# Stores on the ACT queue, group 3 ahead of group 2, and a reordered opening in a chunked-attention and squared-ReLU kernel

## The chip, the cores and the metric

The kernel runs on one core of one Trainium2 chip. The metric is device time in microseconds (us) of one launch, the median of several. A core has five engines that run beside each other, each through its own instructions in order: TensorE (PE, matmul and transpose into PSUM; PEld is its weight load), VectorE (DVE), ScalarE (ACT), GpSimd (POOL) and SyncE (SP). A DMA is issued from an engine's instruction stream (here SP or ACT) and then moved by 16 DMA engines. An instruction that waits for a semaphore holds up everything behind it on its engine.

## The reference

```python
B, H, S, D = 8, 8, 576, 64                      # q, k, v: fp32
q_c, k_c, v_c = (a.reshape(B, H, 9, 64, D) for a in (q, k, v))
scores = D ** -0.5 * q_c @ k_c.swapaxes(-1, -2)  # 64 x 64 per chunk
attn = softmax(scores)
x = (attn @ v_c).reshape(B, H, S, D).transpose(0, 2, 1, 3).reshape(4608, 512)
h = maximum(x @ w_in, 0)                         # w_in 512 x 2048
out = (h * h) @ w_out                            # w_out 2048 x 512, out fp32 4608 x 512
```

Attention stays inside chunks of 64 tokens; a feed-forward network (FFN) with a squared ReLU follows.

## The kernel before

The 4608 tokens are 18 groups of 256, and two groups make a block of 512 (`blocks`, L40): nine blocks, 0 to 8. The order of everything is written out by hand: the program is built in the order in which the Python code calls things, and each engine runs its share of that order.

**Attention of one group** is a chain of steps with short names (L297). For groups 0 to 3, PE transposes q and k (T, `transpose_qk`, or `transpose_qk_early` at the opening), and DVE and then ACT copy the result into `qkT`. From group 4 on POOL casts q and k to bf16 (C, `cast_qk`), and a DMA transpose on SP fills `qkT` (TD, `transpose_qk_dma`, L221). Then come the scores and the exponential on ACT (SC, `scores`), the products with v and the division on DVE (AV, `values`), and the transpose of the result x into `xT` (XT, `transpose_x`; XE and `transpose_x_early` in the opening; from group 6 on it is a DMA transpose on SP, L279).

**FFN of block j** is `ffn_in(j, c, n)`: 16 tiles of columns, called ft here, of four matmuls each (L316), each followed by a ReLU on ACT (`rl`, L322) and a square on DVE (`gT`, L323). Then comes `ffn_out(j)`: four tiles of 128 tokens with 16 matmuls each (L332), and for each a copy `o_sb` on ACT (L339) and a store (L341). Block 0 uses `ffn_out_by_ft` (L352), which can start before all of w_out is there; block 1 does `ffn_in` in two halves of 256 tokens. The matmuls of the FFN write the four PSUM buffers `ps_ffn` in turn, so ft n+4 needs the buffer that the ReLU of ft n has read.

**Interleaving.** Each `yield` of these loops is a slot, counted from 0 in each block: slots 0 to 15 follow the ft of `ffn_in`, then 16 follow `ffn_out` (block 1 has 48 in all). `at(slot, f, g)` puts a step of a later group behind that slot, and one load of q, k or v is issued in each slot in `go_slots` (`loads`). So the scores of groups 2j+2 and 2j+3 stand inside block j, and their loads one or two blocks earlier.

**Queues.** SP issues every load, every DMA transpose and every store, in the order of the program. DMAs take eight completion semaphores, DMAHW0 to DMAHW7, in turn; a DMA is issued only when the DMA that had its semaphore before has landed. That wait stands on the issuing engine.

**Opening.** SP loads q, k and v of groups 0 and 1, then eight slices of w_in and eight of w_out through five staging buffers `w_st`, with a cast on POOL for each (the first slice of w_in as two halves), then groups 2 and 3. `keep_busy(n)` puts n small matmuls without use on PE. PE does T, SC, AV and XE of groups 0 and 1 before block 0.

## Time and profile before

| | us |
|---|---|
| median of 3 runs | 311.0 (310.59 to 311.77) |
| the profiled execution's own time | 308.89 |
| its span, first to last instruction | 307.1 |
| PE busy in the span | 282.2 (92%) |
| ACT busy | 131.1 (43%) |
| DVE busy | 116.0 (38%) |
| POOL busy | 49.9 (16%) |
| mean granted TensorE clock | 0.993 |

All times below are of this one execution, in us from its first instruction; 308.89 - 307.1 = 1.8 us lie outside the span. The blocks begin at 20.95 (block 0), 55.64, 94.31, 127.11, 156.49, 186.41, 216.41, 246.41 and 275.78 (block 8). A row of the timeline gives the start, the time until the last of its instructions ended, engine, line, operation, output<-input, the count and, in brackets, how long the engine sat idle before it and what ended that. "SPq" rows are SP issuing DMAs: their time is that of the issue, not of the transfer. In the rows by windows, "DMA share" is the busy time of 16 DMA engines over the window; it can pass 1.

### The profile page before, as it was taken

The page shows a single profiled execution, that of the slowest core. Times are in us where ns is not written, and L with a number is a line of the kernel's source. Part 1 is how long each engine was busy: PE and PEld are TensorE (multiplying, and loading weights), DVE is VectorE, ACT ScalarE, POOL GpSimd, SP SyncE. Part 2 cuts the span into 40 slices and gives each one's busy share as a digit, 9 for nine tenths or more (in the row PEclk, how much of TensorE's full clock was granted, in tenths as well). Part 3 has the DMA queues.
Part 4 walks back from the last instruction along what each step waited for, and adds up shares of the span by engine and source line. Part 5 has one row for each costly group of instructions (what it writes and reads, how often), then busy time and mean ns, then how long its engine had stood idle before and what let it go on. Part 6 is the DMA issues. An engine that isn't in the chain of part 4 may idle for free.

```text
span 307.1 us, 6400 instructions
## 1 busy us (share of the span) xinstructions
PE 282.2 (92%) x2576; PEld 142.1 (46%) x2610; DVE 116.0 (38%) x246; ACT 131.1 (43%) x225; POOL 49.9 (16%) x68
## 2 busy tenths in 40 slices
PE   2979969899599699999999999999999999999995
PEld 2754434677254244444444444444444444444442
DVE  1348603586053290158026602740284028104400
ACT  1346403666315641374247315631663176226511
POOL 1037830031032050014002200320041000000000
PEclk9999997999999999999999999999999999999999
DMA  7999999897989997997699979999799903210011
GB/s 208 221 308 361 370 236 226 237 202 179 236 189 232 211 216 178 248 198 157 168 244 228 162 172 278 199 142 236 190 216 149 247 36 35 70 68 36 0 68 68
DMA packets 159149, 57.04 MB, mean 186 GB/s; under 512 B 139664, under 2 KB 152464, under 8 KB 159120
## 3 DMA queue, kind: packets, MB, share of 16 engines
q1 hardware_dynamic: 159120, 56.64, 82.1%
q8 instruction: 20, 0.33, 0.5%
q14 instruction: 9, 0.07, 0.1%
HBM read 36.70 MB, written 9.44 MB: 150 GB/s over the span
## 4 chain that ended last, share of the span: by engine, by line
PE 67%; DMA 11%; SPq 7%; DVE 5%; issue 4%; ACT 3%; POOL 1%; ACTq 0%
PE ps_ffn L332 34%; PE ps_ffn L316 27%; DMA w_st<-in_moe_w_in_dram 4%; DMA k_sb<-in_k_dram 3%; DVE gT L323 3%; DMA qkT<-qkb 3%; PE ps_ffn L352 2%; ACT rl L322 2%; DMA w_st<-in_moe_w_out_dram 2%; SPq L101 2%; DVE x L266 2%; SPq L221 1%; PE ps_att L256 1%; SPq L116 1%; SPq L109 1%
## 5 line engine op out<-in xcount | busy, mean ns | idle before, releaser
L316 PE MATMUL ps_ffn<-xT,w_in_bf 128*128 128x512 bf16 (+1 forms) x619 | 128.8, 357 | 1.7 <-ACT xT L201 0.5
L323 DVE TENSOR_TENSOR gT<-rl 128x512 bf16<-128x512 bf16 (+1 forms) x160 | 78.7, 510 | 133.5 <-ACT rl L322 130.9
L332 PE MATMUL ps_ffn<-w_out_bf,gT 128*128 128x512 bf16 x501 | 111.7, 379 | 0.8 <-issue 0.3
L322 ACT ACTIVATE rl<-ps_ffn 128x512 bf16<-128x512 f32 (+1 forms) x160 | 86.9, 558 | 42.8 <-PE ps_ffn L316 33.8
L316 PEld LDWEIGHTS <-w_in_bf 128*128 128x128 bf16 x640 | 60.7, 98 | 59.7 <-DVE xT L293 0.9
L332 PEld LDWEIGHTS <-gT 128*128 128x128 bf16 x512 | 49.8, 98 | 59.1
L339 ACT COPY o_sb<-ps_ffn 128x512 f32<-128x512 f32 x32 | 18.8, 587 | 92.5 <-PE ps_ffn L332 86.8
L214 POOL CAST qkb<-q_sb 128x1024 bf16<-128x1024 f32 x14 | 15.5, 1109 | 156.0 <-DMA q_sb<-in_q_dram 96.8
L266 DVE TENSOR_TENSOR x<-ps_att,rec 128x512 bf16<-128x512 f32 x36 | 24.9, 691 | 1.2
L242 ACT ACTIVATE e<-ps_att 128x1024 bf16<-128x1024 f32 x18 | 17.9, 1026 | 11.0 <-PE ps_att L235 11.0
L214 POOL CAST qkb<-k_sb 128x1024 bf16<-128x1024 f32 x14 | 15.9, 1138 | 1.5 <-DMA k_sb<-in_k_dram 1.2
L352 PE MATMUL ps_ffn<-w_out_bf,gT 128*128 128x512 bf16 x62 | 15.7, 405 | 0.4 <-issue 0.3
L235 PE MATMUL ps_att<-qkT 64*64 64x64 bf16 x576 | 8.1, 200 | 7.2 <-DMA qkT<-qkb 5.7
L263 DVE RECIPROCAL rec<-ps_att 128x8 f32<-128x8 f32 x36 | 7.1, 198 | 16.9 <-PE ps_att L256 16.9
L138 POOL CAST w_in_bf<-w_st 128x1024 bf16<-128x1024 f32 (+1 forms) x9 | 8.7, 966 | 20.3 <-DMA w_st<-in_moe_w_in_dram 20.1
L235 PEld LDWEIGHTS <-qkT 64*64 64x64 bf16 x576 | 6.3, 112 | 12.3 <-DMA qkT<-qkb 6.9
L256 PEld LDWEIGHTS <-e 64*64 64x64 bf16 x576 | 6.6, 107 | 9.1 <-DVE x L266 3.3
L256 PE MATMUL ps_att<-ve_sb,e 64*64 64x65 bf16 x288 | 9.1, 196 | 1.7 <-DVE x L266 1.5
L352 PEld LDWEIGHTS <-gT 128*128 128x128 bf16 x64 | 6.2, 102 | 7.7 <-issue 1.0
L145 POOL CAST w_out_bf<-w_st 128x1024 bf16<-128x1024 f32 x8 | 8.7, 1087 | 3.0 <-DMA w_st<-in_moe_w_out_dram 2.7
L256 PE MATMUL ps_att<-vo_sb,e 64*64 64x65 bf16 x288 | 9.1, 196 | 0.0
L171 ACT COPY qkT<-ps_att 128x512 bf16<-128x512 bf16 x4 | 2.1, 588 | 14.4 <-DVE qkT L171 12.5
(28 smaller groups left out, 47.8 us busy)
## 6 DMA issues: line engine op xcount, KB each, us to landing
out_dram<-o_sb SPq DMA_DIRECT2D x36, 256.0 KB, 2.4
q_sb<-in_q_dram SPq DMA_DIRECT2D x25, 256.0 KB, 4.8
k_sb<-in_k_dram SPq DMA_DIRECT2D x25, 256.0 KB, 5.1
ve_sb<-in_v_dram SPq DMA_DIRECT2D x32, 128.0 KB, 3.9
vo_sb<-in_v_dram SPq DMA_DIRECT2D x32, 128.0 KB, 3.0
w_st<-in_moe_w_out_dram SPq DMA_DIRECT2D x8, 512.0 KB, 5.8
w_st<-in_moe_w_in_dram SPq DMA_DIRECT2D x7, 512.0 KB, 7.3
q_sb<-in_q_dram SPq DMA_DIRECT2D x3, 512.0 KB, 5.4
```

Of the source, the lines that this page charges most:

```text
L138: nc.gpsimd.tensor_copy(out=w_in_bf[:, :, cols], in_=st)
L214: nc.gpsimd.tensor_copy(out=qkb[:, which], in_=qk[g][which].rearrange("p t h d -> p (t h d)"))
L235: nc.tensor.matmul(out=ps[64 * c:64 * c + 64, o0:o0 + 64], lhsT=qkT[64 * a:64 * a + 64, 1, t, hp, cols], rhs=qkT[64 * a:64 * a + 64, 0, t, ...
L242: nc.scalar.activation(out=e.rearrange("p a h t q -> p (a h t q)"), in_=ps, func=AF.Exp, scale=scale)
L256: nc.tensor.matmul(out=ps[64 * p:64 * p + 64, a, hp * (D + 1):(hp + 1) * (D + 1)], lhsT=e[64 * c:64 * c + 64, a, hp, t, :], rhs=vb[64 * c: ...
L266: nc.vector.tensor_tensor(out=x.rearrange("p h a d -> p a h d"), in0=o[:, :, :, 0:D], in1=rec.to_broadcast([128, 2, n_hp, D]), op=ALU.mult)
L316: nc.tensor.matmul(out=h[:, 0:n], lhsT=w_in_bf[:, dt, ft * 128:(ft + 1) * 128], rhs=xT[:, dt, c:c + n], start=(dt == 0), stop=(dt == n_dt ...
L322: nc.scalar.activation(out=rl[:, 0:n], in_=h[:, 0:n], func=AF.Relu)
L323: nc.vector.tensor_tensor(out=gT[:, ft, c:c + n], in0=rl[:, 0:n], in1=rl[:, 0:n], op=ALU.mult)
L332: nc.tensor.matmul(out=o_ps, lhsT=gT[:, ft, tt * 128:(tt + 1) * 128], rhs=w_out_bf[:, ft, :], start=(ft == 0), stop=(ft == n_ft - 1))
L339: nc.scalar.copy(out=o_sb, in_=o_ps)
L352: nc.tensor.matmul(out=o_ps[tt], lhsT=gT[:, ft, tt * 128:(tt + 1) * 128], rhs=w_out_bf[:, ft, :], start=(ft == 0), stop=(ft == n_ft - 1))
```

## The change

Stores are issued from ACT (`nc.scalar.dma_start`) instead of SP. Block 1 is [3, 2] instead of [2, 3], so group 3 is loaded and handled first; the rows of the stores and the pieces of odd v follow. The first two slices of w_in are loaded from the ACT queue, as whole slices, between the transposes of group 1 and AV of group 0; the cast of slice 0 is still in two halves. AV of group 0 stands before SC of group 1, there are 42 instead of 66 idle matmuls, the k half of group 1 is copied on ACT instead of DVE, and `transpose_x_early` copies its second half on DVE. In block 1, 17 instead of 20 loads stand before the DMA transposes of groups 4 and 5. In block 2, SC, AV and XT of groups 6 and 7 stand two slots later (`d` from 2 to 4).

```diff
--- before.py
+++ after.py
@@ -37,7 +37,8 @@
     n_ft = d_ff // 128
     GT = 256
     n_grp = n_tokens // GT
-    blocks = [[g, g + 1] for g in range(0, n_grp, 2)]
+
+    blocks = [[0, 1], [3, 2]] + [[g, g + 1] for g in range(4, n_grp, 2)]
     FIRST_DMA_T = 4
     FIRST_DMA_X = 6
     BT = GT * max(len(b) for b in blocks)
@@ -116,7 +117,7 @@
             yield lambda t=t, p=p, m=m, b=b, s=s: nc.sync.dma_start(
                 out=v_even[g % NV][p:p + m, t, :, 0:D],
                 in_=v[b, 0::2, s:s + m, :].rearrange("h s d -> s h d"))
-        for n in ([0] if g == 0 else []) + [2 * g + 1, 2 * g + 2]:
+        for n in {0: [0, 1, 2], 2: [5], 3: [6, 7, 8]}.get(g, [2 * g + 1, 2 * g + 2]):
             lo, hi = max(0, 128 * n - 64), min(n_tokens, 128 * n + 64)
             p = lo - (128 * n - 64)
             for b, s, m in segments(lo, hi - lo):
@@ -129,13 +130,14 @@
         for f in pieces:
             f()
 
-    def load_w_in(c0, n=256):
-        cols = slice(c0, c0 + n)
-        st = wst_pool.tile([128, 1024], FP32, name="w_st")
-        st = st[:, 0:n_dt * n].rearrange("p (a f) -> p a f", a=n_dt)
-        nc.sync.dma_start(
-            out=st, in_=moe_w_in[:, cols].rearrange("(a p) f -> p a f", p=128))
-        nc.gpsimd.tensor_copy(out=w_in_bf[:, :, cols], in_=st)
+    def load_w_in(i, eng=nc.sync, n_cast=1):
+        cols = slice(i * 256, (i + 1) * 256)
+        st = wst_pool.tile([128, 1024], FP32, name="w_st").rearrange("p (a f) -> p a f", a=n_dt)
+        eng.dma_start(out=st, in_=moe_w_in[:, cols].rearrange("(a p) f -> p a f", p=128))
+        n = 256 // n_cast
+        for c in range(0, 256, n):
+            nc.gpsimd.tensor_copy(
+                out=w_in_bf[:, :, i * 256 + c:i * 256 + c + n], in_=st[:, :, c:c + n])
 
     def load_w_out(i):
         st = wst_pool.tile([128, 1024], FP32, name="w_st").rearrange("p (a f) -> p a f", a=2)
@@ -198,7 +200,8 @@
                 out=psb[:, hp * 128:(hp + 1) * 128],
                 in_=x[:, hp].rearrange("p a d -> p (a d)"),
                 identity=ident)
-        nc.scalar.copy(
+        copy = nc.vector.tensor_copy if t else nc.scalar.copy
+        copy(
             out=xTs[j][:, :, c + t * 128:c + (t + 1) * 128],
             in_=psb[:, 0:512].rearrange("p (h t) -> p h t", h=n_hp))
 
@@ -337,8 +340,8 @@
                 if ft == n_ft - 1:
                     o_sb = ffn_pool.tile([128, d_model], FP32, name="o_sb", bufs=4)
                     nc.scalar.copy(out=o_sb, in_=o_ps)
-                    t0 = blocks[j][0] * GT + tt * 128
-                    nc.sync.dma_start(out=out[t0:t0 + 128, :], in_=o_sb)
+                    t0 = blocks[j][tt // 2] * GT + tt % 2 * 128
+                    nc.scalar.dma_start(out=out[t0:t0 + 128, :], in_=o_sb)
                 if ft % 4 == 3:
                     yield
 
@@ -364,8 +367,8 @@
                 mm(tt, ft)
             o_sb = ffn_pool.tile([128, d_model], FP32, name="o_sb", bufs=4)
             nc.scalar.copy(out=o_sb, in_=o_ps[tt])
-            t0 = blocks[j][0] * GT + tt * 128
-            nc.sync.dma_start(out=out[t0:t0 + 128, :], in_=o_sb)
+            t0 = blocks[j][tt // 2] * GT + tt % 2 * 128
+            nc.scalar.dma_start(out=out[t0:t0 + 128, :], in_=o_sb)
             yield
 
     def pieces(grps):
@@ -378,27 +381,26 @@
     transpose_qk_early(0, nc.scalar.copy)
     keep_busy(8)
     SC(0)
+    keep_busy(6)
+    transpose_qk_early(1, nc.scalar.copy)
+    load_w_in(0, nc.scalar, 2)
+    load_w_in(1, nc.scalar)
+    AV(0)
+    SC(1)
     keep_busy(8)
-    transpose_qk_early(1, nc.vector.tensor_copy)
-    keep_busy(10)
-    SC(1)
-    keep_busy(10)
-    AV(0)
-    keep_busy(16)
     XE(0)
+    keep_busy(6)
     AV(1)
     keep_busy(10)
     XE(1)
     keep_busy(4)
 
-    load_w_in(0, 128)
-    load_w_in(128, 128)
-    for i in range(1, 8):
-        load_w_in(i * 256)
+    for i in range(2, 8):
+        load_w_in(i)
     for i in range(8):
         load_w_out(i)
-    go(pieces([2]))
-    go(pieces([3]))
+    for g in blocks[1]:
+        go(pieces([g]))
 
     for j, grps in enumerate(blocks):
         nxt = blocks[j + 1] if j + 1 < len(blocks) else []
@@ -411,13 +413,13 @@
         if j == 0:
             loads, go_slots = iter(()), []
             for slot, f in ((24, T), (26, SC), (28, AV), (30, XT)):
-                at(slot, f, 2)
+                at(slot, f, nxt[0])
             phases = [ffn_in(0, 0, 512), ffn_out_by_ft(0)]
         elif j == 1:
-            go_slots = [*range(20), *range(34, 48)]
+            go_slots = [*range(17), *range(34, 48)]
             loads = itertools.chain(pieces(nxt), pieces(far))
             for slot, f in ((1, T), (4, SC), (7, AV), (12, XT)):
-                at(slot, f, 3)
+                at(slot, f, grps[1])
             for i, g in enumerate(nxt):
                 for slot, f in ((22 + 4 * i, C), (27 + 4 * i, TD), (36, SC), (38 + 2 * i, AV),
                                 (42 + 2 * i, XT)):
@@ -425,7 +427,7 @@
             phases = [ffn_in(1, 0, 256), ffn_in(1, 256, 256), ffn_out(1)]
         else:
             loads, go_slots = pieces(far), range(32)
-            d = 2 if j == 2 else 0
+            d = 4 if j == 2 else 0
             if j == 2:
                 go_slots = [*range(10), *range(18, 32)]
             for i, g in enumerate(nxt):
```

Three places show what this does to the order. First ACT in the opening, from its first copy to the first xT copy. Before:

```order
L171 COPY qkT<-ps_ffn 128x512 x2
L242 ACTIVATE e<-ps_att 128x1024 x2
L201 COPY xT<-ps_ffn 128x4x128 x4
L322 ACTIVATE rl<-ps_ffn 128x512 x16
L171 COPY qkT<-ps_att 128x512 x2
```

With the change:

```order
L173 COPY qkT<-ps_ffn 128x512 x2
L245 ACTIVATE e<-ps_att 128x1024
L173 COPY qkT<-ps_ffn 128x512 x2
L136 DMA w_st<-in_moe_w_in_dram 128x4x256 x2
L245 ACTIVATE e<-ps_att 128x1024
L204 COPY xT<-ps_ffn 128x4x128 x2
L325 ACTIVATE rl<-ps_ffn 128x512 x16
```

The two loads of w_in now stand between the copies of group 1 and its exponential.

Second, SP in the second half of block 1, around the DMA transposes of groups 4 and 5 (`qkT<-qkb x2`); the rows ahead of them load v of group 5. Before:

```order
L116 DMA ve_sb_90<-in_v_dram 128x4x64 x2
L123 DMA vo_sb_95<-in_v_dram 128x4x64
L123 DMA vo_sb_96<-in_v_dram 128x4x64
L109 DMA q_sb<-in_q_dram 128x8x64
L109 DMA k_sb<-in_k_dram 128x8x64
L109 DMA q_sb<-in_q_dram 64x8x64
L221 DMA_TRANSPOSE qkT<-qkb 128x16x128 x2
L109 DMA k_sb<-in_k_dram 64x8x64
L341 DMA out_dram<-o_sb 128x512
```

With the change:

```order
L117 DMA ve_sb_90<-in_v_dram 128x4x64 x2
L124 DMA vo_sb_95<-in_v_dram 128x4x64
L124 DMA vo_sb_96<-in_v_dram 128x4x64
L224 DMA_TRANSPOSE qkT<-qkb 128x16x128 x2
L110 DMA q_sb<-in_q_dram 128x8x64
L110 DMA k_sb<-in_k_dram 128x8x64
```

Three loads of group 6 moved behind the transposes, and the store left SP.

Third, the end of block 4 and the start of block 5 on ACT, and what stands on SP at that time, with the semaphores that each row waits for (Activation is ACT's own, so a store waits for its copy). ACT before:

```order
L339 COPY o_sb<-ps_ffn 128x512 [waits DMAHW2_49,PE_49]
L339 COPY o_sb<-ps_ffn 128x512 [waits DMAHW3_49,PE_49]
L339 COPY o_sb<-ps_ffn 128x512 [waits DMAHW4_49,PE_49]
L322 ACTIVATE rl<-ps_ffn 128x512 [waits DVE_49,PE_49] x5
L242 ACTIVATE e<-ps_att 128x1024 [waits PE_49] x2
```

ACT with the change:

```order
L342 COPY o_sb<-ps_ffn 128x512 [waits DMAHW3_49,PE_49]
L344 DMA out_dram<-o_sb 128x512 [waits DMAHW2_49,Activation_49]
L342 COPY o_sb<-ps_ffn 128x512 [waits PE_49]
L344 DMA out_dram<-o_sb 128x512 [waits DMAHW5_49,Activation_49]
L325 ACTIVATE rl<-ps_ffn 128x512 [waits DVE_49,PE_49] x5
```

SP with the change, from the DMA transposes of groups 12 and 13 on:

```order
L224 DMA_TRANSPOSE qkT<-qkb 128x16x128 [waits DMAHW1_49,Pool_49]
L224 DMA_TRANSPOSE qkT<-qkb 128x16x128 [waits DMAHW2_49,Pool_49]
L110 DMA q_sb<-in_q_dram 128x8x64 [waits DMAHW3_49]
L110 DMA k_sb<-in_k_dram 128x8x64 [waits DMAHW5_49]
L110 DMA q_sb<-in_q_dram 128x8x64 [waits DMAHW6_49]
L110 DMA k_sb<-in_k_dram 128x8x64 [waits DMAHW0_49]
L110 DMA q_sb<-in_q_dram 128x8x64 [waits DMAHW1_49]
L110 DMA k_sb<-in_k_dram 128x8x64 [waits DMAHW3_49]
```

A store now stands between the last copy and the first ReLU of block 5. It waits for DMAHW5, which the first k load of these SP rows (the second load) had before it; the store ahead of it waits for DMAHW2, that of the second transpose. The SP loads in turn wait for semaphores that earlier stores had.

## The prediction

> **What bounds the kernel now.** I read the page first, then PE's timeline with its idle times, then windows of the suspicious stretches, then SP's timeline.
>
> ```profile
> span 307.1 us, 6400 instructions
> PE 282.2 (92%) x2576; PEld 142.1 (46%) x2610; DVE 116.0 (38%) x246; ACT 131.1 (43%) x225; POOL 49.9 (16%) x68
> PE   2979969899599699999999999999999999999995
> PEclk9999997999999999999999999999999999999999
> ```
>
> PE is the bound, and from slice 16 on (123 us) it is full to the end. What can be won stands in the first 15 slices. PE's timeline names the waits there; these are all that are over 0.7 us between 20.95 and the end:
>
> ```profile
> 44.25 0.64 PE L162 MATMUL ps_att<-ident,q_sb 128*64 128x128 bf16 x16 [1.35 <-DMA q_sb<-in_q_dram]
> 45.96 0.64 PE L162 MATMUL ps_att<-ident,k_sb 128*64 128x128 bf16 x16 [1.07 <-DMA k_sb<-in_k_dram]
> 80.44 0.45 PE L235 MATMUL ps_att<-qkT 64*64 64x64 bf16 x32 [1.45 <-DMA qkT<-qkb]
> 82.37 0.45 PE L235 MATMUL ps_att<-qkT 64*64 64x64 bf16 x32 [1.49 <-DMA qkT<-qkb]
> 101.37 0.45 PE L235 MATMUL ps_att<-qkT 64*64 64x64 bf16 x32 [1.01 <-DMA qkT<-qkb]
> 103.52 0.44 PE L235 MATMUL ps_att<-qkT 64*64 64x64 bf16 x32 [1.70 <-DMA qkT<-qkb]
> ```
>
> Three places: 2.42 us in block 0 (q and k of group 2 have not landed), 2.94 in block 1 (the DMA transposes of groups 4 and 5), 2.71 in block 2 (those of groups 6 and 7). Each ends on a DMA, so I ask of each: was the data late because the DMA engines were full, or because SP issued late? The windows (PE, PEld, DVE, ACT, POOL busy, then clock, DMA share, GB/s) answer:
>
> ```profile
> 14.30:18.00 3.70, 3.34 (x126) 2.79 (x114) 1.70 (x4) 1.78 (x3) 0.60 (x1) 1.00 0.78 208
> 20.00:40.00 20.00, 19.41 (x94) 8.97 (x95) 12.26 (x16) 10.21 (x18) 14.68 (x14) 1.00 1.06 363
> 46.98:50.39 3.41, 3.41 (x40) 1.35 (x39) 0.95 (x2) 1.12 (x3) 0.00 (x0) 0.50 1.15 292
> 52.80:56.50 3.70, 3.70 (x27) 2.06 (x26) 2.15 (x4) 1.92 (x5) 0.00 (x0) 1.00 0.59 218
> 56.50:66.00 9.50, 8.12 (x152) 6.33 (x151) 6.38 (x17) 5.46 (x15) 2.12 (x2) 1.00 1.13 220
> ```
>
> The engines are full from 20 to 40 us and from 56.5 to 66, with holes at 14.3 to 18 and at 52.8 to 56.5. SP's timeline shows what made the second hole, and what stood ahead of the transposes:
>
> ```profile
> 49.02 1.74 SPq L123 DMA_DIRECT2D vo_sb<-in_v_dram  x2
> 52.84 3.87 SPq L368 DMA_DIRECT2D out_dram<-o_sb  x4
> 56.75 0.43 SPq L109 DMA_DIRECT2D q_sb<-in_q_dram  x1
> ...
> 72.20 0.50 SPq L109 DMA_DIRECT2D q_sb<-in_q_dram  x1
> 72.75 0.78 SPq L109 DMA_DIRECT2D k_sb<-in_k_dram  x1
> 73.57 2.42 SPq L109 DMA_DIRECT2D q_sb<-in_q_dram  x1
> 76.11 3.94 SPq L221 DMA_TRANSPOSE qkT<-qkb  x2
> ...
> 94.96 0.36 SPq L341 DMA_DIRECT2D out_dram<-o_sb  x1
> ...
> 97.07 4.05 SPq L221 DMA_TRANSPOSE qkT<-qkb  x2
> ```
>
> From 50.76 to 56.75 SP issues no load: the four stores of block 0 wait for their copies, and the loads of groups 4 and 5 queue behind them.
>
> **The change part by part.**
>
> *Block 1.* SP no longer stops for stores, so the loads of group 4 can start near 50.8 instead of 56.75: 5.9 us earlier. Three loads (0.50 + 0.78 + 2.42 = 3.70 us of issue) leave the place ahead of the transposes. Together 9.6 us: the transpose that let PE go at 82.37 would land near 72.8, and PE asks for it at 80.44 - 1.45 = 79.0, or 77.6 with the gain of block 0. Should the DMA engines and not SP set the pace, the hole alone gives 3.70 x (1 - 0.59/1.13) = 1.8 us, and the 640 KB less ahead give 2.9 more at 220 GB/s: 4.7, and 82.37 - 77.6 - 0.45 = 4.3 are needed. Gain **2.9**; the lower bound is 0.4 (the hole alone, 1.8 in all, of which block 0 has 1.4), the upper 2.94. What is late next is nothing near: the cover left is 4.8 us. The loads of group 5 now wait for semaphores of block 0's stores; these land some 2 us after the copies, when SP would be there anyway.
>
> *Block 2.* The scores move from slot 6 to slot 8, eight matmuls of 512 columns later. PE's row for this place gives their length:
>
> ```profile
> 94.15 6.21 PE L316 MATMUL ps_ffn<-xT,w_in_bf 128*128 128x512 bf16 x27
> ```
>
> 6.21/28 = 0.222 us each (28 in the program, one record missing), so 1.8 us. The pair of transposes before was issued 2.8 us after the block's start at 94.31, behind the last store of block 1 (94.96) and three loads, and let PE go 6.45 us after its issue (103.52 - 97.07). Now the loads ahead of the pair wait only for the semaphore of the store before that one, some 4 us older, so I put the pair at 2 us after the block's start; it lands at about 8.4. The second SC asks for it at 36 x 0.222 + 0.45 = 8.4. Gain 2.71 less 0.1, **2.6**; bounds 1.8 (the slots alone) and 2.71. AV and XT move with it; the xT they make is not wanted before block 3, over 10 us later.
>
> *Opening and block 0.* The opening's own chain is shorter: the q copies of group 1 no longer carry the k copies on DVE behind them (1.2 us), 24 idle matmuls go, AV(0) fills a wait. The rows of its end and of block 0's waits:
>
> ```profile
> 12.46 11.59 SPq L136 DMA_DIRECT2D w_st<-in_moe_w_in_dram  x9
> 17.40 1.37 POOL L138 CAST w_in_bf<-w_st 128x512 bf16<-128x512 f32 x2 [15.21 <-DMA w_st<-in_moe_w_in_dram]
> 20.95 13.97 PE L316 MATMUL ps_ffn<-xT,w_in_bf 128*128 128x512 bf16 x62 [0.45 <-ACT xT L201]
> ...
> 48.02 1.07 ACT L171 COPY qkT<-ps_att 128x512 bf16<-128x512 bf16 x2 [12.46 <-DVE qkT L171]
> 49.65 0.64 PE L235 MATMUL ps_att<-qkT 64*64 64x64 bf16 x32
> ```
>
> An earlier block 0, though, only waits longer at 44.25: q and k there are the last of a queue that runs full (share 1.06). They come earlier only by the hole of 14.3 to 18 us, 3.70 x (1 - 0.78/1.06) = 1.0 us, if the first slices on ACT's queue and five full slices in the staging buffers (two of which held halves) fill it. Group 3 brings the same 1 MB as group 2. So PE goes on at 45.0 instead of 46.0. The half clock of 46.98 to 50.39 follows on these waits; without it the eight matmuls until SC would be done near 48.4 and not 49.6, but SC then waits for the copies that end at 49.09, so it is worth some 0.6; at a little over even odds, with shorter waits, 0.4. Gain **1.4**. Upper bound 2.42 + 0.6 = 3.0. Lower bound: the w_in slices share the engines with the last v loads and ACT holds the exponential of group 1 while it issues (0.4 to 1.3 us each by SP's rows, 0.43 for one load, 11.59/9 for these). Block 0 would start later, but up to 2.4 us of that is absorbed by the two waits; so -0.5.
>
> The row of 20 to 40 us speaks of full engines, and the Trainium skill, "DMA: Bandwidth & Descriptors", section "Issuing engines are not separate DMA queues", has the rule that speaks against this change: DMAs from ACT, SP and GpSimd run on the same 16 engines, so issuing from several saves issue time alone. By that rule the hole is not filled by a second queue, and the sum below would be 1.0 less; by the hole's row it is filled. The rule does not touch blocks 1 and 2, where SP waited and the engines had room (0.59).
>
> *Stores on ACT.* Thirty-six issues leave SP and stand on ACT.
>
> ```profile
> L341 SPq DMA_DIRECT2D out_dram<-o_sb x32: 332/376/595, 80.8 to 304.1; - x32
> SPq L341 <- ACT o_sb L339: 48.7, 16, 16.9
> ```
>
> 0.38 us each (min/median/max), 13.7 in all, in stretches where ACT has only copies to do. On ACT an issue on a busy queue is not in the trace: between 0.33 and the 2.42 of a load. Behind a block's last store stand the ReLUs of the next block; PE has four buffers, so it stops only when the first ReLU ends after four ft. The worst place is the end of block 4, where that store waits for the second load behind the transposes:
>
> ```profile
> 167.97 0.69 DVE L266 TENSOR_TENSOR x<-ps_att,rec 128x512 bf16<-128x512 f32 x1
> 170.48 4.01 SPq L279 DMA_TRANSPOSE xT<-x  x2
> 180.96 4.72 SPq L221 DMA_TRANSPOSE qkT<-qkb  x2
> 187.95 0.72 SPq L109 DMA_DIRECT2D k_sb<-in_k_dram  x1
> k_sb<-in_k_dram SPq DMA_DIRECT2D x1, 256.0 KB, 5.1
> 186.45 0.59 ACT L339 COPY o_sb<-ps_ffn 128x512 f32<-128x512 f32 x1 [2.87 <-PE ps_ffn L332]
> 186.41 4.33 PE ps_ffn L316 x20
> ```
>
> Before, that load was issued at 187.95 and landed 5.1 later. Without the store between (0.5), and with SP ahead by up to 2.6 us (x is there at 167.9, not earlier), the transposes end between 182.6 and 185.2 instead of 185.7, the load lands 5.6 later, 188.2 to 190.8, and the first ReLU ends 1.0 after that: 189.2 to 191.8. PE stops at 186.41 + 4 x 0.865 = 189.9. So 0 to 1.9; SP nearer to the early end: **-0.2**.
>
> Sum: 2.9 + 2.6 + 1.4 - 0.2 = 6.7. The profiled execution took 308.89, so 302.2; that one lies 2.1 under the median of the runs, 311.0, and for the median I forecast **304.3**.
>
> **The rivals.** (1) *The DMA engines, not the queue, set the pace.* The full windows speak for it, the holes against it. By it the opening's hole stays, so block 0 gains 0.4; block 1 still 2.9, by fewer bytes ahead; block 2 1.8 by the slots; less 0.2: 311.0 - 4.9 = 306.1. The skill's rule above is this rival.
>
> (2) *Stores hold ACT at block ends.* If SP falls behind PE by x instead of leading, because its loads now wait for stores that wait for loads, the last stores of blocks 3, 4 and 5 wait. At block 4 PE stops 1.9 + x; at blocks 3 and 5, whose stores wait for a transpose and for a load just landed by then, I let it stop x - 2. With x = 5 that is 6.9 + 3 + 3 = 12.9, and 311.0 - 6.9 + 12.9 = 317, slower. It decides from about x = 3, where 4.9 + 1 + 1 eat all that is gained. For it: SP's rows stand close together from 97 on. Against it: SP loses 1.6 us of issues per block and 48.7 us of waits for copies.
>
> (3) *The waits only move.* The loads of groups 4 to 7 now wait for semaphores of the stores, so the transposes end as late as before: 311.0 - 1.4 + 0.2 = 309.8, no change. Against it: in block 1 seventeen loads stand ahead of the transposes and only three of them wait for a store, all of block 0.
>
> (4) *All goes well.* The upper bounds: 2.94 + 2.71 + 3.0 = 8.7, 302.3.
>
> **How the numbers follow.** Forecast (303 to 305.5) 0.47; rival 1 (305.5 to 307.5) 0.18; rival 2 0.16, of it 0.05 under 309, 0.04 near no change and 0.07 slower; rival 3 0.09; rival 4 (under 303) 0.10. About 0.5%, 1.6 us, is what a measurement of this kernel can tell from no change. Faster by more: 0.47 + 0.18 + 0.05 + 0.10 = 0.80; within 0.5%: 0.09 + 0.04 = 0.13; slower 0.07. The range reaches from rival 4 over rival 1 and the mild end of rival 2, 302.0 to 309.0, and leaves out 0.20.
>
> **What would show it.** Right: no wait of L238 on qkT in block 1 and under 0.5 us in block 2; the first load of group 4 issued before 52; DMA share near 1 at 14 to 18; a wait for k of group 3 of 1 to 2 us still there. Wrong: ACT idle at a store while the first ReLU of a block is due; block 0 starting after 22; the second transpose of block 2 still landing over 9 us after the block's start.

## The result, and the profile after

| | before | changed |
|---|---|---|
| median of 4 runs, us | 311.3 (310.59 to 311.77) | 301.7 (301.32 to 303.97) |
| profiled execution, us | 308.89 | 301.32 |
| its span, us | 307.1 | 299.5 |

The ratio is 0.971 (95% interval 0.966 to 0.976): 9 to 10 us less by the runs, 7.6 by the two traces. Forecast were 304.3 and a range from 302.0; the median lies 0.3 under that range. Ratios, here and below, leave out executions more than 1.5% above the fastest of their kernel (among them one each of 372, 1194 and 1641 us, of u_order, shift and u_opening), while the medians are of all executions.

From the page after: the span, the busy times, and PE and its clock in 40 slices.

```profile
span 299.5 us, 6352 instructions
PE 280.2 (94%) x2552; PEld 141.7 (47%) x2586; DVE 115.0 (38%) x246; ACT 130.5 (44%) x225; POOL 49.0 (16%) x68
PE   2889988789999999899999999999999999999995
PEclk9959999999999999999999999999999999999999
```

The half clock of slice 6 (slices count from 0) is gone; one now stands in the opening (slice 2), though not in the changed kernel's second trace, that of the run after_again. PE's timeline after has these waits over 0.5 us from block 0 on; I add the row of the scores of groups 4 and 5, which have none:

```profile
44.59 0.64 PE L164 MATMUL ps_att<-ident,k_sb 128*64 128x128 bf16 x16 [0.77 <-DMA k_sb<-in_k_dram]
58.26 0.22 PE L238 MATMUL ps_att<-qkT 64*64 64x64 bf16 x4 [1.31 <-ACT qkT L173]
66.66 7.16 PE L319 MATMUL ps_ffn<-xT,w_in_bf 128*128 128x256 bf16 x64 [0.93 <-DVE xT L296]
78.07 0.82 PE L238 MATMUL ps_att<-qkT 64*64 64x64 bf16 x64
99.16 0.45 PE L238 MATMUL ps_att<-qkT 64*64 64x64 bf16 x32 [0.63 <-DMA qkT<-qkb]
125.96 0.45 PE L238 MATMUL ps_att<-qkT 64*64 64x64 bf16 x32 [0.70 <-DMA qkT<-qkb]
```

Six waits on a DMA before, 8.1 us (2.42 + 2.94 + 2.71); three now, 2.1 us. Two waits in block 1, on ACT and on DVE, are longer. They had 0.64 and 0.17 us before:

```profile
59.76 0.22 PE L235 MATMUL ps_att<-qkT 64*64 64x64 bf16 x4 [0.64 <-ACT qkT L171]
67.51 7.16 PE L316 MATMUL ps_ffn<-xT,w_in_bf 128*128 128x256 bf16 x64 [0.17 <-DVE xT L293]
```

Where the 7.6 us come from, by the start of each block's first matmul in PE's timelines (this table and its rows for the experiments below are worked out from those starts; the last number of a row is what is left from block 3 to the end; by them blocks 2 to 8 of the kernel before begin 0.16 us earlier than the list ahead of the prediction has it):

```
                     block 0 starts   block 0   block 1   block 2   block 3 to end
before                        20.95     34.69     38.50     32.80           180.15
changed                       20.77     32.71     36.75     30.17           179.10
changed, second trace         19.61     33.10     36.22     31.79           179.27
u_stores                      20.94     31.21     36.82     32.47           178.26
u_win                         20.36     32.72     36.20     33.39           178.22
u_order                       20.31     34.22     35.88     30.15           178.95
u_slots                       20.83     31.89     39.09     32.71           179.68
u_opening_2                   21.00     32.81     36.34     32.44           179.51
o_opening                     20.63     35.95     39.90     32.58           178.24
o_stores                      20.96     37.28     36.17     34.17           179.02
best                          19.49     32.50     34.65     30.37           179.69
```

So 0.2 + 2.0 + 1.8 + 2.6 + 1.0 = 7.6. A single trace moves by one to two microseconds in a block: the changed kernel's second trace has 1.6 more in block 2 and nearly the same end. A difference under that is read here only with the row that makes it.

### The profile page after: what moved, and what is told of

It reads as the page before. It is cut to its first block, busy times and chain, and to the rows that moved or that the text cites. A ratio compares the mean times of both kernels' runs of the same rounds, so it can differ in the third digit from the quotient of the medians.

```text
span 299.5 us, 6352 instructions
## 1 busy us (share of the span) xinstructions
PE 280.2 (94%) x2552; PEld 141.7 (47%) x2586; DVE 115.0 (38%) x246; ACT 130.5 (44%) x225; POOL 49.0 (16%) x68
## 4 chain that ended last, share of the span: by engine, by line
PE 70%; DMA 15%; SPq 7%; DVE 2%; ACT 2%; issue 2%; POOL 1%; ACTq 0%
PE ps_ffn L335 33%; PE ps_ffn L319 32%; DMA qkT<-qkb 3%; DMA w_st<-in_moe_w_in_dram 3%; DMA k_sb<-in_k_dram 3%; DMA w_st<-in_moe_w_out_dram 2%; DMA ve_sb<-in_v_dram 2%; PE ps_att L259 2%; SPq L224 2%; PE ps_att L238 2%; SPq L102 2%; DMA out_dram<-o_sb 1%; SPq L282 1%; SPq L124 1%; SPq L117 1%
## 5 line engine op out<-in xcount | busy, mean ns | idle before, releaser
L326 DVE TENSOR_TENSOR gT<-rl 128x512 bf16<-128x512 bf16 (+1 forms) x160 | 77.9, 504 | 131.8 <-ACT rl L325 128.3
L217 POOL CAST qkb<-q_sb 128x1024 bf16<-128x1024 f32 x14 | 14.8, 1061 | 146.0 <-DMA q_sb<-in_q_dram 122.8
L217 POOL CAST qkb<-k_sb 128x1024 bf16<-128x1024 f32 x14 | 15.3, 1091 | 4.1 <-DMA k_sb<-in_k_dram 4.1
```

Of the source, the lines that this page charges most:

```text
L217: nc.gpsimd.tensor_copy(out=qkb[:, which], in_=qk[g][which].rearrange("p t h d -> p (t h d)"))
L326: nc.vector.tensor_tensor(out=gT[:, ft, c:c + n], in0=rl[:, 0:n], in1=rl[:, 0:n], op=ALU.mult)
```

## The experiments

Names with u_ are the changed kernel with one part undone, names with o_ the kernel before with one part alone. Ratios are to the kernel before, of runs on the same chip, with 95% intervals:

| kernel | median, us | ratio |
|---|---|---|
| after_again | 300.9 | 0.9705 (0.9668 to 0.9742) |
| u_stores | 302.0 | 0.9655 (0.9609 to 0.9701) |
| u_win | 302.8 | 0.9686 (0.9646 to 0.9726) |
| u_order | 302.0 | 0.9698 (0.9650 to 0.9747) |
| u_slots | 304.2 | 0.9742 (0.9700 to 0.9785) |
| u_opening, u_opening_2 | 306.8, 304.8 | 0.9775 (0.9714 to 0.9836), 0.9774 (0.9729 to 0.9819) |
| o_opening | 308.3 | 0.9892 (0.9853 to 0.9931) |
| o_stores | 308.5 | 0.9917 (0.9873 to 0.9961) |
| b_fill | 311.8 | 0.9987 (0.9939 to 1.0036) |
| shift | 302.2 | 0.9729 (0.9686 to 0.9772) |
| best | 298.5 | 0.9640 (0.9580 to 0.9699) |

### Stores: undone, and alone

```diff
# u_stores                      (o_stores: the other way round, in the kernel before)
-                    nc.scalar.dma_start(out=out[t0:t0 + 128, :], in_=o_sb)
+                    nc.sync.dma_start(out=out[t0:t0 + 128, :], in_=o_sb)
```

> The changed kernel with its 36 stores issued by SP again; all else as changed (301.7 us median). Theory A (SP stopping at stores is what made the transposes late, and SP's lead is also what moved POOL's casts off the squares ahead of AV in blocks 4 to 6): blocks 4 to 6 lose about 0.6 us each again (1.8), block 1 and block 2 get transpose waits of 1 to 2 us together, block 1 gets back 0.7 (no store ahead of its first ReLU): about 303.5. Rival B (the fewer loads ahead and the later slots carry blocks 1 and 2, the stores only cost ACT time): block 1 gets 0.7 to 1.4 back and nothing else moves: 300.5 to 301.

> The kernel before with its 36 stores on ACT and nothing else. Theory A (as in my prediction: SP's stop at 50.8 to 56.8 us is what makes the transposes of groups 4 and 5 late): their waits in block 1, 2.9 us, shrink to under 1, and 309.5 to 310.5. Rival B (as the changed kernel with stores on SP showed: the first load of group 4 is issued 2 to 3 us earlier, but the transposes are issued at the same time, since the DMA engines set the pace; ACT's store delays the first ReLU of block 1 by 0.7): 312 to 313, no gain.

Undone, the stores cost nothing: 0.9655 against 0.9705, if anything the other way, and the intervals overlap. Alone they bring 0.8% (2.6 us). The traces show how the first can be; what brings the 0.8% they do not show. First u_stores: SP from block 0's stores to the transposes of groups 4 and 5, then PE at the scores of groups 4 to 7.

```profile
49.34 3.87 SPq L371 DMA_DIRECT2D out_dram<-o_sb  x4
53.26 0.43 SPq L110 DMA_DIRECT2D q_sb<-in_q_dram  x1
...
69.27 5.90 SPq L224 DMA_TRANSPOSE qkT<-qkb  x2
```

```profile
75.39 0.45 PE L238 MATMUL ps_att<-qkT 64*64 64x64 bf16 x32 [0.22 <-DMA qkT<-qkb]
77.20 0.45 PE L238 MATMUL ps_att<-qkT 64*64 64x64 bf16 x32 [1.36 <-DMA qkT<-qkb]
98.21 0.44 PE L238 MATMUL ps_att<-qkT 64*64 64x64 bf16 x32 [1.30 <-DMA qkT<-qkb]
100.20 0.45 PE L238 MATMUL ps_att<-qkT 64*64 64x64 bf16 x32 [1.55 <-DMA qkT<-qkb]
```

In the changed kernel the same two SP rows read:

```profile
50.63 0.50 SPq L110 DMA_DIRECT2D q_sb<-in_q_dram  x1
...
69.17 4.19 SPq L224 DMA_TRANSPOSE qkT<-qkb  x2
```

In the changed kernel SP starts these loads 2.6 us earlier and comes to the transposes 0.1 us earlier. The lead is gone by the seventh load (issued at 59.30 and, in u_stores, at 59.18), in a stretch where the DMA engines are full (share 0.97 to 1.20 in windows of 2 us from 52 to 60). From 64.5 to 68.6 SP issues seven loads of v back to back at a share of only 0.61 and 0.65 (windows 64 to 66 and 66 to 68): there its own issue sets the pace, with the stores or without. When the second transpose of block 1 (that of group 5) had landed, and when PE was ready for it, worked out from SP's issues, their times to landing (in the changed kernel the second is issued at 71.67 and takes 5.7) and PE's rows less their waits:

```
                        pair issued from   second landed   PE asks for it
before                             76.11           82.33            80.88
o_stores                           73.75           81.98            82.64
changed                            69.17           77.35            78.34
changed, second trace              68.61           76.29            77.18
u_stores                           69.27           77.15            75.84
u_slots                            71.52           79.98            79.82
u_order                            69.90           77.99            78.64
u_opening_2                        69.98           77.23            78.38
```

In u_stores that transpose lands no later than in the changed kernel. PE waits for it all the same, since it asks 2.5 us earlier, mostly because block 1 starts 1.3 us earlier and its waits on ACT and DVE are 1.0 shorter. Block 1 is as long as in the changed kernel (36.82), with other waits in it. In block 2 the waits come back as well (2.85 us, against 0.63, or 1.68 in the second trace).

What stores cost on ACT: ACT in the changed kernel at the end of block 0, then the same place before:

```profile
53.84 0.58 ACT L369 COPY o_sb<-ps_ffn 128x512 f32<-128x512 f32 x1 [0.82 <-PE ps_ffn L355]
54.97 0.34 ACTq L371 DMA_DIRECT2D out_dram<-o_sb  x1
55.35 0.66 ACT L325 ACTIVATE rl<-ps_ffn 128x256 bf16<-128x256 f32 x2 [0.93 <-DMA out_dram<-o_sb]
```

```profile
55.76 0.59 ACT L366 COPY o_sb<-ps_ffn 128x512 f32<-128x512 f32 x1 [0.72 <-PE ps_ffn L352]
56.35 0.82 ACT L322 ACTIVATE rl<-ps_ffn 128x256 bf16<-128x256 f32 x2
```

The last store waits for the semaphore of an earlier store until 54.97, and the first ReLU of block 1 starts 0.93 us behind the copy instead of at once. The squares, the copies of q and k of the block's own second group and its scores follow: 1.31 us of wait instead of 0.64. In u_stores it is 0.65 again. The delay depends on which DMA had the semaphore: in the changed kernel it was the first store of the same block, which landed at 54.89, 0.5 us after the last copy's end. In u_order and o_stores, whose stores are on ACT too, a load of v had it that had landed 2.7 and 3.7 us before the copy ended, and PE waits 0.64 and 0.65.

In o_stores the transposes of groups 4 and 5 are on time:

```profile
82.37 0.71 PE L235 MATMUL ps_att<-qkT 64*64 64x64 bf16 x64
```

That looks like my forecast for this edit, but not by its mechanism. The first load of group 4 is issued 4.2 us earlier than before (52.55), yet the first transpose lands at 80.39, as before, and the second 0.35 earlier. PE does not wait because it comes later: block 1 starts at 58.23 instead of 55.64, behind a block 0 with 6.8 us at half clock, and loses 1.80 us to DVE on the way (see "The casts beside the squares"). The traced execution took 309.39 us, no less than the 308.89 before, so where the 0.8% of the runs come from stays open.

### Opening: undone, and alone; and w_in on SP

```diff
# u_opening, u_opening_2: load_w_in, XE's copies and the order of before
-    keep_busy(6)
-    transpose_qk_early(1, nc.scalar.copy)
-    load_w_in(0, nc.scalar, 2)
-    load_w_in(1, nc.scalar)
+    keep_busy(8)
+    transpose_qk_early(1, nc.vector.tensor_copy)
+    keep_busy(10)
+    SC(1)
+    keep_busy(10)
     AV(0)
-    SC(1)
-    keep_busy(8)
+    keep_busy(16)
...
+    load_w_in(0, 128)
+    load_w_in(128, 128)
# u_win: new order, w_in on SP
-    load_w_in(0, nc.scalar, 2)
-    load_w_in(1, nc.scalar)
+    load_w_in(0, nc.sync, 2)
+    load_w_in(1)
```

> The changed kernel with the opening of before (order, 66 idle matmuls, copies, every slice of w_in on SP, slice 0 as two halves in two buffers); stores, group order and slots as changed. Theory A (the opening carries the 2.2 us by which block 1 starts earlier: fuller DMA engines at 14 to 18 us, and no half clock in block 0): 303.5 to 304, waits for q and k of the first group of block 1 of 2 us or more. Rival B (the engines are full anyway; the gain of block 0 comes from elsewhere): within 0.5 of 301.7.

> The changed kernel with the opening of before once more, for its trace (the profiled execution of the first time took 1641 us and says nothing of this kernel). Theory A (the old opening's cost is a later block 0 and longer waits for q and k of group 3): block 0 starts near 21, the two waits ahead of T of group 3 are 3 us or more, the transposes of groups 4 and 5 are 2 us or more later than with the new opening. Rival B (it is the clock): the waits are as with the new opening, and a stretch at half clock of 3 us or more stands in block 0 or 1.

> The kernel before with the new opening alone (order, 42 idle matmuls, copies on both engines, first two slices of w_in on ACT's queue). In the runs so far the changed kernel without the new opening stood near 306.5 and with it at 301.7. Theory A (the opening is worth some 4 us by itself: block 0 and everything on the DMA queues start earlier and the waits of blocks 1 and 2 move along with it): 307.5 to 308.5, against 312 for the kernel before. Rival B (an earlier block 0 only waits longer, for q and k of group 2 in block 0 and for the transposes of groups 4 and 5): 310.5 to 311.5, and the waits before T of group 2 together 3 us or more.

> The changed kernel with the first two slices of w_in on SP, at the same place of the program; the rest of the new opening stays. Theory A (the second queue fills the hole of 14 to 18 us): block 0's k wait grows by about 1 us, 302.7. Rival B (the hole is filled by five whole slices in the buffers instead of halves, or by the order, and the queue does not matter): 301.7 within 0.5.

The trace read here is that of u_opening_2. Undoing the opening costs 0.7% against after_again (0.9774 and 0.9705, some 2 us; the intervals overlap a little), and alone it brings 1.1% (3.4 us). The trace of u_opening_2 has no half clock in the blocks, so that isn't the cause; block 0 starts 0.2 to 1.4 us later than in the changed kernel's traces, and both transposes of groups 6 and 7 are late again:

```profile
99.17 0.45 PE L236 MATMUL ps_att<-qkT 64*64 64x64 bf16 x32 [1.09 <-DMA qkT<-qkb]
100.97 0.45 PE L236 MATMUL ps_att<-qkT 64*64 64x64 bf16 x32 [1.35 <-DMA qkT<-qkb]
```

My theory's place, the waits in block 0, is not where the cost is: block 0 is as long as in the changed kernel (32.81). Against the changed kernel's first trace the cost lies in block 2 (2.3 us), against its second in the start of block 0 (1.4) and then in block 2 (0.65); two traces don't settle which. The queue of w_in doesn't matter for the time: u_win is 0.2% from after_again, inside the intervals. Windows of the hole of before, in the changed kernel and in u_win (PE, PEld, DVE, ACT, POOL busy, clock, DMA share, GB/s):

```profile
14.30:18.00 3.70, 3.11 (x86) 2.71 (x84) 1.88 (x4) 1.54 (x2) 0.00 (x0) 0.60 1.05 298
52.80:56.50 3.70, 3.70 (x54) 2.69 (x53) 1.34 (x4) 1.46 (x4) 0.00 (x0) 1.00 1.09 307
```

```profile
14.30:18.00 3.70, 3.70 (x88) 3.37 (x77) 1.30 (x4) 1.61 (x2) 0.04 (x1) 0.56 0.89 269
```

With both slices on SP two thirds of the hole are filled by GB/s (269, between 208 before and 298), two fifths by DMA share (0.89, between 0.78 and 1.05). That part is the work of the new order and of whole slices in the five buffers, which no run here tells apart. In time, a second issuing engine alone brought nothing that these runs can tell. This agrees with the rule quoted in the prediction (the Trainium skill, "DMA: Bandwidth & Descriptors", "Issuing engines are not separate DMA queues").

### Order of groups 2 and 3 undone

```diff
-    blocks = [[0, 1], [3, 2]] + [[g, g + 1] for g in range(4, n_grp, 2)]
+    blocks = [[g, g + 1] for g in range(0, n_grp, 2)]
```

> The changed kernel with group 2 ahead of group 3 as before; all else as changed. Theory A (the parts have to add up: 9.6 in all, some 4.5 by the opening, 2.5 by the slots, nothing by the stores, so 2 to 3 by the order; group 2 crosses the border of two batches and its q and k take four DMAs, the last of which landed latest): 304, waits for q and k in block 0 of 2 us or more. Rival B (both groups bring the same 1 MB ahead of T): 301.7 within 0.6.

The time is the same (0.9698), though not the place. PE in block 0 of u_order:

```profile
43.90 0.64 PE L164 MATMUL ps_att<-ident,q_sb 128*64 128x128 bf16 x16 [1.65 <-DMA q_sb<-in_q_dram]
45.63 0.64 PE L164 MATMUL ps_att<-ident,k_sb 128*64 128x128 bf16 x16 [1.10 <-DMA k_sb<-in_k_dram]
```

Its waits are 2.75 us where the changed kernel has 0.77 (1.20 in its second trace). Block 0 is 1.1 to 1.5 us longer, and later blocks give it back (block 1's wait on ACT is 0.64 instead of 1.31). "Within 0.6" was right, but its reason was not: the order does shorten the waits of block 0, and the sum is unchanged.

### Slots undone

```diff
-            go_slots = [*range(17), *range(34, 48)]
+            go_slots = [*range(20), *range(34, 48)]
-            d = 4 if j == 2 else 0
+            d = 2 if j == 2 else 0
```

> The changed kernel with 20 loads ahead of the transposes in block 1 and SC, AV, XT of groups 6 and 7 two slots earlier, as before. Theory A (from 57 us on the DMA engines set the pace; the second transpose of block 1 landed only 0.7 us ahead of its use): three loads more are 2 to 3 us more ahead of it, a wait of about 2 in block 1, and 1.8 more in block 2: 305.5. Rival B (SP set the pace and the cover in block 1 is near the 4.8 us that I forecast): only block 2 loses, 1.8: 303.5.

0.9742, some 1.2 us more than after_again (the intervals overlap). PE at the scores of groups 4 to 7:

```profile
79.37 0.45 PE L238 MATMUL ps_att<-qkT 64*64 64x64 bf16 x32
80.03 0.45 PE L238 MATMUL ps_att<-qkT 64*64 64x64 bf16 x32 [0.21 <-DMA qkT<-qkb]
...
99.85 0.45 PE L238 MATMUL ps_att<-qkT 64*64 64x64 bf16 x32 [1.84 <-DMA qkT<-qkb]
101.55 0.44 PE L238 MATMUL ps_att<-qkT 64*64 64x64 bf16 x32 [1.25 <-DMA qkT<-qkb]
```

The wait in block 1 is 0.21 us and not the 2 of theory A, but its transposes are late as theory A has it: the second lands at 79.98, 2.6 us later than in the changed kernel. PE hardly waits because it asks 1.5 us later, after a stretch at half clock (58.99 to 62.40) and waits of 1.88 us on ACT and 1.34 on DVE in the same block. Rival B's reason, a cover near 4.8 us, is refuted by the table under the stores: in the changed kernel the second transpose lands 1.0 us ahead of its use. Block 2's waits are 2.46 longer than in the first trace (1.84 + 1.25 - 0.63), and 1.4 longer than in the second, where 1.8 were expected.

### The casts beside the squares

Blocks 4, 5 and 6 were 0.6 us longer before than after, though the only edit there is the stores' queue, and u_stores, with the old queue, has no such loss. DVE and POOL in block 4 of the kernel before, and PE at AV:

```profile
165.67 1.30 DVE L323 TENSOR_TENSOR gT<-rl 128x512 bf16<-128x512 bf16 x1 [0.44 <-ACT rl L322]
```

```profile
165.66 1.04 POOL L214 CAST qkb<-q_sb 128x1024 bf16<-128x1024 f32 x1 [21.32 <-DMA q_sb<-in_q_dram]
```

```profile
168.71 0.22 PE L256 MATMUL ps_att<-ve_sb,e 64*64 64x65 bf16 x2 [0.37 <-DVE x L266]
```

A square that begins with a cast on POOL takes 1.30 us; the division behind it is late and with it the second half of AV. In all thirteen traces, of the squares of 128 x 512 after 115 us, none that ran without a cast (or with one for under a third of its time) took over 0.427 us, and the others took up to 1.3 (medians from 0.69 to 1.25). The Trainium skill, "SBUF — State Buffer", section "Who interferes with whom", says that a DVE instruction with two SBUF inputs contends with a GpSimd instruction that reads SBUF, and that the port pair they share is an exclusive lock. The trace agrees as far as it goes: the square began 0.01 us behind the cast and ended 0.27 behind the cast's end, though its 1.30 us are less than 1.04 + 0.42.

Block 1 has the same after the change: the cast of group 5's q runs at 64.02 instead of 68.22, and the square of 128 x 256 beside it takes 1.12 us, where those without a cast take 0.28. The copy of xT that PE waits 0.93 us for comes later by that. In o_stores two such squares (1.16 and 1.12) make it 1.80 us; the changed kernel's second trace has no such wait. I tried to move the casts of blocks 3 and on:

```diff
-            loads, go_slots = pieces(far), range(32)
+            loads, go_slots = pieces(far), range(2 if j > 2 else 0, 32)
```

> The changed kernel with the loads of blocks 3 on begun two slots (1.7 us) later, so that POOL's casts run 1.7 us later in each block. Theory A (blocks 4 to 6 of the kernel before lost 0.6 us each because a POOL cast ran beside the squares on DVE just ahead of AV and made them last 1.2 instead of 0.42 us; the changed kernel's casts run some 1.4 us earlier in the block and miss them): the wait of 0.4 ahead of the second half of AV comes back in two or more blocks, with a cast beside the squares there: 302.9 to 303.9. Rival B (the squares are late for another reason): 301.7 within 0.5 and no such wait.

The casts didn't move, since the edit did not delay the loads. SP around the first load of block 3's slots, first in the changed kernel and then in shift:

```profile
122.49 1.13 SPq L124 DMA_DIRECT2D vo_sb<-in_v_dram  x2
123.67 0.50 SPq L110 DMA_DIRECT2D q_sb<-in_q_dram  x1
```

```profile
122.89 1.18 SPq L124 DMA_DIRECT2D vo_sb<-in_v_dram  x2
124.13 0.50 SPq L110 DMA_DIRECT2D q_sb<-in_q_dram  x1
```

In both, SP goes on to this load at once (0.05 and 0.06 us behind the loads ahead of it): a slot is a place in the program's order, and moving the load by two slots put no other SP instruction ahead of it. Block 3 starts at 120.40 and at 121.33, so the load stands 0.5 us earlier in the block, not 1.7 later, and the first cast 0.7 earlier (131.51 and 131.76). No wait at AV came back. The experiment therefore decided nothing. The AV wait appears in two of blocks 3 to 6 of u_opening_2, in one of u_order and of o_stores, in three of before, and in none of the others, b_fill among them, whose blocks 3 to 8 are programmed as before. No edit goes with it, so the 1.8 us of blocks 4 to 6 are luck of where the casts fell in the traced executions, and not a gain of an edit that I can name.

### The clock, and the changed kernel once more

```diff
# b_fill: T of group 2 in the kernel before (raw is the PSUM tile that the transposes write)
+            if g == 2:
+                for _ in range((22, 14)[which]):
+                    nc.tensor.matmul(out=raw[:, which * 512:which * 512 + 128],
+                                     lhsT=ident, rhs=ident, start=True, stop=True)
             transpose_paired(g, which, ps[:, which * 1024:(which + 1) * 1024])
```

> The kernel before with idle matmuls in T of group 2: 22 ahead of the q transposes and 14 ahead of those of k, where PE waited 1.35 and 1.07 us for the loads. They write PSUM that the transposes overwrite. Theory A (a wait of PE of about a microsecond is what lets the granted clock fall to half for 3.4 us or more behind it): no half clock behind T of group 2, mean clocks at 0.994 and above, 1.5 to 2 us off the time: ratio 0.994 to 0.995. Rival B (the clock falls by itself, or by load): clocks stay near 0.989 and the ratio is 1.00.

> The changed kernel once more, beside the other runs of this series and on their chip. Theory A (the change is worth 9.6 us by medians, 7.6 by the two traces; the rest are stretches at half clock, of which the kernel before has one more in a typical execution than in the traced one): ratio 0.969 to 0.973, mean granted clock of its executions above that of the kernel before by 0.003 or more. Rival B (the 2 us are the luck of one traced execution and no clock): ratio near 0.975, clocks alike.

The ratio of after_again is 0.9705, as at first, and as theory A has it; the clocks are not. Over the executions that are compared the mean granted clock is 0.9907, against 0.9891 of the kernel before: 0.0016 more, where theory A asked for 0.003. The ratios rest on 32 executions of the kernel before whose mean granted clock is known, of which three have 0.994: 307.9 to 308.2 us. Those with 0.987 to 0.989 have a median of 311.2, those with 0.984 or less 312.0. The profiled execution that I worked from (308.89) had 0.993. A stretch of 3.41 us at half clock takes 0.0056 off the mean, so it was one of the few with a single stretch, and its block 0, 34.69 us, is the shortest of the four traces of kernels built on that one (35.95 in o_opening, 36.50 in b_fill, 37.28 in o_stores). The changed kernel shows no such relation: 301.82 at 0.998, 300.42 at 0.993, 300.67 at 0.987. And a second stretch of 3.41 us loses about 1.7 us of matmuls at half clock, where the medians lie 3 us apart: the clock goes with the time of the kernel before, and doesn't explain all of it.

b_fill had 0.994 or more in four of the seven executions that its ratio rests on, yet its time is that of the kernel before within the interval. In its traced execution, with no half clock in the blocks, the loads were later: PE still waited behind the idle matmuls.

```profile
46.05 0.64 PE L162 MATMUL ps_att<-ident,q_sb 128*64 128x128 bf16 x16 [0.93 <-DMA q_sb<-in_q_dram]
```

u_order speaks against a simple rule: 2.75 us of waits at the same place, and no half clock. That waits lead to the half clock is thus not shown, and what it costs is open.

### A version that uses this

```diff
# best = changed kernel and
-            nc.scalar.dma_start(out=out[t0:t0 + 128, :], in_=o_sb)      (ffn_out_by_ft: block 0)
+            nc.gpsimd.dma_start(out=out[t0:t0 + 128, :], in_=o_sb)
-            d = 4 if j == 2 else 0
+            d = {2: 5, 3: 1}.get(j, 0)
# and 8 idle matmuls ahead of the k transposes of group 3, as in b_fill
```

> The changed kernel with what its trace asks for: the four stores of block 0 on POOL's queue (POOL is idle there), SC, AV and XT one slot later in blocks 2 and 3, and eight idle matmuls ahead of the k transposes of group 3. Theory A (the first ReLU of block 1 was 0.66 late behind the last store on ACT, the rest of block 1's waits 0.3, the transposes were 0.63 and 0.70 late in blocks 2 and 3): 2 us less, ratio 0.963 to 0.965. Rival B (the DMA engines set the pace and each wait only moves): ratio as the changed kernel, 0.97, with waits of as much further on.

298.5 us, ratio 0.9640, as theory A has it; beside it on the same chip after_again had 300.9 and 0.9705. The intervals overlap a little, so the trace has to say what it rests on. PE in block 1, PE in block 2, and POOL with the store that stood on ACT:

```profile
56.11 0.22 PE L243 MATMUL ps_att<-qkT 64*64 64x64 bf16 x4 [0.64 <-ACT qkT L173]
63.19 7.05 PE L324 MATMUL ps_ffn<-xT,w_in_bf 128*128 128x256 bf16 x63 [0.17 <-DVE xT L301]
96.24 0.45 PE L243 MATMUL ps_att<-qkT 64*64 64x64 bf16 x32 [0.44 <-DMA qkT<-qkb]
```

```profile
52.98 0.54 POOL L376 DMA_DIRECT2D out_dram<-o_sb  x1 [0.77 <-ACT o_sb L374]
```

Both of block 1's waits are at their values of before, and its transposes are on time too: 34.65 us, the shortest block 1 of all traces. Block 2 waits 0.44 us, and block 3 not at all. Block 5 lost 1.15 us, by the mechanism that the prediction priced for that place. ACT, then PE, at the end of block 4:

```profile
177.09 0.59 ACT L347 COPY o_sb<-ps_ffn 128x512 f32<-128x512 f32 x1 [3.96 <-PE ps_ffn L324]
179.47 0.34 ACTq L349 DMA_DIRECT2D out_dram<-o_sb  x1
179.91 2.56 ACT L330 ACTIVATE rl<-ps_ffn 128x512 bf16<-128x512 f32 x5 [2.23 <-PE ps_ffn L324]
```

```profile
180.56 1.02 PE L324 MATMUL ps_ffn<-xT,w_in_bf 128*128 128x512 bf16 x4 [1.15 <-ACT rl L330]
```

The stores of blocks 1 to 8 were not tried on POOL: the casts of groups 6 and 7 stand behind block 1's on that queue.

## Why the prediction was right or wrong

**Block 0 and the opening: right in direction, too low.** Forecast 1.4 (bounds -0.5 to 3.0), measured 0.2 + 2.0. The hole filled (share 0.78 to 1.05), in good part by the whole slices and the order and not by the second queue, and it is not what carries block 0: with the old opening and group 3 first (u_opening_2) block 0 takes 32.81 us, as in the changed kernel. "Group 3 brings the same 1 MB as group 2", costed at nothing, is the step that was mis-sized: with group 2 first the waits for q and k are 2.75 us, with group 3 first 0.77 and 1.20. "The half clock follows on these waits" is not shown: it is gone from block 0, but u_order has the waits and no half clock, and in the first trace a stretch came into the opening, which I hadn't foreseen.

**Block 1: right in its waits, wrong in the sum.** The 2.94 us of waits for the transposes went. The block gained 1.75 (2.28 in the second trace). The step that failed is "what is late next is nothing near: the cover left is 4.8 us": it was 1.0. The first load of group 4 came 6.1 us earlier (5.9 were forecast), and with the three loads' 3.7 that makes 9.8. Of these 6.9 were left when the pair of transposes was issued, and 5.0 when the second landed, because the full engines held up the loads and the pair took 8.2 us from its issue to land instead of 6.2. The alternative that I worked out beside it, with the DMA engines as the pace (4.7 us), was near; that SP's own issue sets the pace again behind them was in neither. And two prices were missing: the store ahead of block 1's first ReLU (1.31 - 0.64 = 0.67), which I had priced at block ends 3 to 5 alone, and casts that meet the squares (0.93 - 0.17 = 0.76; not in the second trace).

**Block 2: the forecast number, partly by luck.** Forecast 2.6, measured 2.6 (1.0 in the second trace). The pair was issued 2.1 us after the block's start, as forecast, and landed at 8.9 instead of 8.4. So the waits fell from 2.71 to 0.63 and not to 0.1, 2.1 us; of the rest 0.28 is a wait of AV on DVE that no term had. In the second trace the pair came 3.5 us after the start and landed at 9.95. The experiments add that it takes the slots, the stores and the opening together: each one undone has waits of 2.4 to 3.1 us there, against 0.6 and 1.7 in the changed kernel's two traces.

**Stores on ACT: the place was right.** Forecast -0.2 (0 to -1.9) at the end of block 4. In the profiled execution, whose rows stand here, the first ReLU came late and PE just didn't stop; in the second trace it stopped 0.39 us, in best 1.15, and in u_slots 0.91 at the end of block 3:

```profile
180.22 0.58 ACT L342 COPY o_sb<-ps_ffn 128x512 f32<-128x512 f32 x1 [2.87 <-PE ps_ffn L335]
182.05 0.34 ACTq L344 DMA_DIRECT2D out_dram<-o_sb  x1
182.49 2.64 ACT L325 ACTIVATE rl<-ps_ffn 128x512 bf16<-128x512 f32 x5 [1.69 <-DMA k_sb<-in_k_dram]
```

The k load that the store waits for landed at 181.97, 2.0 us after block 5's start, where the kernel before had it 6.8 after: the early end of what I worked out. The rival "stores hold ACT at block ends" named this mechanism; its x = 5 never came, since SP runs ahead of PE and not behind. What I had wrong was the weight of the stores: they carried the reasoning for block 1, and undone they cost nothing.

**Blocks 3 to 8: not in the sum.** 1.0 us: 1.8 by the casts' place in blocks 4 to 6, which is luck, less 0.9 in block 3, where one of the transposes of groups 8 and 9 now comes 0.70 late.

**From the sum to the median.** 6.7 were forecast against 7.6 by trace, which is 0.9 of the miss. The other 1.7 is the step "that one lies 2.1 under the median of the runs": I carried this distance over to the changed kernel, whose profiled execution lies 0.4 under its median. The 2.1 belonged to that one execution of the kernel before; that its clock is the reason is likely for part of it and not shown.

So the direction and the places were right, and that 6.7 and 7.6 lie close is in part luck: 1.2 too much for block 1 stands against 0.8 too little for block 0 and 1.0 that no term had.

Of the rivals, (1) had the cause in part: in the changed kernel full engines hold up the loads from 53 to 60 us, and the loads ahead of the transposes count (three more make the second land 2.6 us later), but its 306.1 was too slow. (3) is refuted by the missing waits in block 1. The time lies where I had put (4), under 303 with a chance of 0.10, though not by its mechanism: blocks 1 and 2 stayed under their upper bounds.

Of the signs, an early first load of group 4 (50.63), no wait in block 1 and a share near 1 in the hole came; the wait in block 2 is 0.63, over the 0.5. Two signs of being wrong came too: ACT stood at a store while block 1's first ReLU was due (0.93 us), and in the second trace block 2's second transpose landed over 9 us after the block's start.

## What to carry to other kernels

Several edits that bring the same data earlier relative to its use don't add: undone one at a time, the parts here cost some 3 us together (the opening 2, the slots 1), of the 9 to 10 that all bring, and the opening and the stores alone bring 3.4 and 2.6. So neither way gives a part its share. A wait that vanishes is no proof that its data came earlier: write down when the data landed and when it was asked for, as in the table under the stores, before naming an edit as the cause. When an issuing engine is relieved, first ask whether the DMA engines or the engine set the pace behind the hole, and then what the earlier data will start (a cast beside another engine's work, a store that waits for a semaphore ahead of a due instruction). And one profiled execution is no typical one: compare its time and clock with the other runs before a distance between them is carried over.

## What was not expected of the hardware

The squares on DVE took 0.42 us alone and up to 1.3 beside a cast on POOL. Stretches of half clock of 3.4 us, or twice that, stood near waits of PE far shorter than they: behind 1.35 + 1.07 us before, behind three of 0.2 to 0.4 us in the changed kernel's opening; u_order had waits of 1.65 and 1.10 us in block 0 and none. Seven loads of v, issued by SP back to back, kept the DMA engines only 0.6 busy. The four stores that POOL issued took 0.54 to 0.68 us of it each, where ACT took 0.34 to 0.75 in the changed kernel.
